# Gate-u weight jobs moved behind the first period and onto GpSimd's queue

## The chip, the cores and the metric

The kernel runs on one core of a Trainium2 chip. The metric is device time in microseconds for one execution. The engines are TensorE (PE, matrix products; its weight loads are listed apart as PEld), VectorE (DVE), ScalarE (ACT), GpSimd (POOL) and SyncE (SP). SP does nothing here but issue transfers; GpSimd issues some too. An engine works through its own instructions strictly in the order in which the program has them, and waits where an operand isn't ready.

## What is computed

A linear-attention layer with a delta rule, then a gated mixing block, then a channel block. Cut to what matters:

```python
# attention: per batch and head (4 x 8), 768 tokens, head dim 48
for t in range(S):
    y[t] = q[t] @ state
    state = state + beta[t] * outer(k_n[t], v[t] - k_n[t] @ state)
# x = y of all heads side by side: [4, 768, 384]
h = gelu(x @ w_in)                  # 384 x 1024
u, v = h[..., :512], h[..., 512:]   # "gate u" and "gate v"
v_n = layernorm(v) * g_ln
v_s = w_sg @ v_n + b_sg             # over the tokens
x = x + (u * v_s) @ w_out
xk, xr = shifted mixes of x         # mu_k, mu_r
out = sigmoid(xr @ w_r) * ((relu(xk @ w_k) ** 2) @ w_v)
```

Products that need it are done as three or four products of a high and a low part in the rounded type fp32r. So every weight matrix has to be rounded on the chip into a high and a low part before PE can use it.

## The kernel before

The attention part runs over 144 points in six periods of 24 (g = 0 to 5, 128 tokens each). A "run" is a slot of the attention and three points: after the attention steps of the slot (st_rq, st_d, st_n, st_s, st_y) `tick()` is called three times. For each period the chunk's triangular systems have to be solved first: `solver(g + 1)` is a long chain of DVE operations (from the transpose L360 over L355 and L393 to the last transpose L440, which writes DT) that runs while PE works on period g. `couple` (L456) is the first product of a new period that reads DT. `st_d` (L521) reads r, which DVE makes (L475) from what st_rq left; `st_n` reads u (ACT L526); `st_s` (L549) reads the SQ and sw0 tiles that ACT fills at L540 and L555. `warm` matmuls (L726) fill places where PE would have nothing to do.

In the gaps of DVE, ACT and POOL the weights are rounded by jobs. `narrow` is the body of a job for one block of 128 rows by 256 columns (192 for w_out): the load of `raw` (L160, issued on SP), ACT L164, four DVE operations L169, L171, L173, L175 in the tile `na`, POOL L177, ACT L120 for the high part, POOL L123 for the low part. `raw` has three buffers and `na` two, so the third job's L169 needs the first job's L123. `resident` makes such jobs for w_in, whose results stay in SBUF: six of gate v (wiv) and six of gate u (wiu), in that order. `scratch` makes the jobs of the other weights, whose results go to DRAM by one more transfer (L202) and are loaded later through GpSimd's queue (L212).

The order of all engines is made when the program is built: `background(t)` deals out a budget of DVE time at each point among three kinds of streams, layer-norm steps, the solver and jobs, in proportion to the shares in `SHARE` (one triple for the lead-in, one for the first period, one for the rest). `start_job(lead)` takes the next job off the list, issues its load and lets its operations begin `lead` points later. `tick()` starts a job where n, the point within the period, is a multiple of EVERY or, from point LATE on, of 2, as long as fewer than RUN jobs run and the point is below LASTP; and as long as w_in jobs are left (`len(jobs) > n_rest`) it starts them at any point. What is left at the end of the attention part runs beside the mixing block. `after(n, f)` puts a piece n points later. After the attention part PE does the mixing block (about 336 to 504 us) and then the channel block (504 to 745).

Of the kernel before, what the change touches and what calls it, by code (L numbers as in the profile page):

```python
# [9 lines left out]
U32 = mybir.dt.uint32  # L10
# [8 lines left out]
FF = 1024  # L19
HF = 512  # L20
P = 128
# [5 lines left out]
CW = 256  # L27
NPRE = 1.2
LJ = 2
LJ5 = 6  # L30
LJ0 = 7
SLOT0 = 3.3
LOW0 = 1
# [6 lines left out]
RUN = (3, 2, 3)  # L40
SUMS = (0,)
EVERY = 6
LATE = 100
PUT = 2
JLAG = 2
BUDGET = 1.62
# [5 lines left out]
LNW = 1  # L52
LAGX = 6
LAGE = (7, 11)
LASTP = 134
FROM = 125
LAGU = 5
COST = dict(rq=1.05, d=0.8, n=0.8, s=0.85, y=1.1)
INST = dict(rq=128, d=128, n=64, s=64, y=64)
PACE = 0.0157  # L60
SHARE = ((1, 12, 1), (1, 4, 1), (2, 8, 2))
NRAW = 3
NNA = 2
PD = 2
# [9 lines left out]
def vw(t, off, dims):  # L74

    a = t[:]
    return bass.AP(a.tensor, a.offset + off, [list(a.ap[0])] + [list(d) for d in dims])
# [9 lines left out]
def fused_kernel(  # L87
# [17 lines left out]
    nc = tc.nc  # L105
    V, A, G, T = nc.vector, nc.scalar, nc.gpsimd, nc.tensor
# [3 lines left out]
    stg = ctx.enter_context(tc.tile_pool(name="stg", bufs=2))  # L110
# [6 lines left out]
    def split(eng_hi, eng_lo, src, hi, lo):  # L117

        if eng_hi is A:
            A.activation(hi, src, AF.Copy)  # L120
        else:
            eng_hi.tensor_scalar(hi, src, 1.0, None, op0=ALU.mult)
        eng_lo.tensor_tensor(lo, src, hi.bitcast(F32), op=ALU.subtract)  # L123
# [27 lines left out]
                T.matmul(pt, lhsT=a, rhs=b, start=(i == 0), stop=(i == n - 1))  # L151
                i += 1

    def narrow(dram, i, j, hi, lo, cw=CW, pool=stg, lag=JLAG, parts=None):

        w = CW if pool is stg else cw
        raw = pool.tile([P, 2 * w], U32, name="raw", bufs=NRAW)
        nc.sync.dma_start(out=raw[:, :2 * cw], in_=dram[i * P:(i + 1) * P, j:j + cw].bitcast(U32))  # L160
        w_lo = vw(raw, 0, [(2, cw)])
        w_hi = vw(raw, 1, [(2, cw)])
        yield 0
        yield 0, lambda: A.activation(w_lo.bitcast(I32), w_lo, AF.Copy, scale=2.0 ** -29)  # L164
        a = pool.tile([P, w], U32, name="na", bufs=NNA if pool is stg else 2)[:, :cw]
        af = a.bitcast(F32)
        t1 = cw / 1920 + 0.16
        t2 = cw / 960 + 0.16
        V.tensor_scalar(a, w_hi, 0x7FFFFFFF, None, op0=ALU.bitwise_and)  # L169
        yield t1  # L170
        V.tensor_scalar(af, af, E_LO_F, E_HI_F, op0=ALU.max, op1=ALU.min)  # L171
        yield t1
        V.tensor_scalar(a, a, 3, 0x3FFFFFFF, op0=ALU.logical_shift_left, op1=ALU.bitwise_and)  # L173
        yield t1
        V.scalar_tensor_tensor(a, w_hi, 0xC0000000, a, op0=ALU.bitwise_and, op1=ALU.bitwise_or)  # L175
        yield t2
        G.tensor_tensor(a.bitcast(I32), a.bitcast(I32), w_lo.bitcast(I32), op=ALU.add)  # L177
        if hi is None:
            hi, lo = (raw[:, e * cw:e * cw + cw].bitcast(F32R) for e in range(2))
            parts.append(raw[:, :2 * cw].bitcast(F32).rearrange("p (x n) -> p x n", x=2))  # L180
        yield lag, lambda: split(A, G, af, hi, lo)

    def resident(dram, pool, name, nblk, n, j0=0, j1=None):


        j1 = j1 or n
        hi = pool.tile([P, nblk, j1 - j0], F32R, name=name + "_hi", bufs=1)
        lo = pool.tile([P, nblk, j1 - j0], F32R, name=name + "_lo", bufs=1)
        return hi, lo, [lambda i=i, j=j: narrow(dram, i, j, hi[:, i, j - j0:j - j0 + CW],
                                                lo[:, i, j - j0:j - j0 + CW], lag=0)  # L190
                        for i in range(nblk) for j in range(j0, j1, CW)]

    def scratch(dram, name, nblk, n, cw=CW, pool=stg):

        d = dp.tile([nblk, P, 2, n], F32, name=name + "_d")

        def job(i, j):
            parts = []
            yield from narrow(dram, i, j, None, None, cw, pool, parts=parts)

            def put():
                nc.sync.dma_start(out=d[i, :, :, j:j + cw], in_=parts[0])  # L202

            yield PUT, put

        return d[:, :, 0], d[:, :, 1], [lambda i=i, j=j: job(i, j) for i in range(nblk) for j in range(0, n, cw)]
# [12 lines left out]
    wo_dh, wo_dl, jobs = scratch(w_out, "wo", 4, DM, DM // 2)  # L219
    wk_dh, wk_dl, j1 = scratch(w_k, "wk", 3, FF)  # L220
    jobs += j1
    n_rest = len(jobs)
    fp = tc.tile_pool(name="fp", bufs=2)
    fl = ctx.enter_context(ExitStack())
    fp = fl.enter_context(fp)
# [23 lines left out]
    with ExitStack() as at:  # L249
        ap1 = at.enter_context(tc.tile_pool(name="ap1", bufs=1, side="right"))  # L250
        ap2 = at.enter_context(tc.tile_pool(name="ap2", bufs=2, side="right"))
        ps1 = at.enter_context(tc.tile_pool(name="ps1", bufs=1, space=PSUM))
        ps2 = at.enter_context(tc.tile_pool(name="ps2", bufs=2, space=PSUM))
        wv_hi, wv_lo, in_jobs = resident(w_in, fp, "wiv", 3, FF, HF, FF)
        wu_hi, wu_lo, j1 = resident(w_in, fp, "wiu", 3, FF, 0, HF)
        in_jobs += j1

        NKT = 5
# [61 lines left out]
        def gram(g, parts=((0, 64),)):  # L320

            GL = GLs[g] = GLb[g % 3]

            def half(i, c0, c1, j):
                t = kT[2 * g + i // 2]
                if j == 0:
                    GDs["ps"] = bank()
                gps = GDs["ps"]
                for p in range(4 * j, 4 * j + 4):
                    u = (i % 2) * 8 + p  # L330
                    for h in range(2):
                        r = 64 * (1 - h)
                        T.matmul(gps[r:r + 32, p, c0:c1], lhsT=t[r:r + 64, u, 0:32],  # L333
                                 rhs=t[r:r + 64, u, c0:c1], start=True, stop=True)
                        T.matmul(gps[r + 32:r + 64, p, c0:c1], lhsT=t[r:r + 64, u, 32:64],  # L335
                                 rhs=vw2(t, r, 64, u * C + 32 - c0, [(-32, (c1 - c0) // 32), (1, 32)]),
                                 start=True, stop=True)
                if j:
                    for x, c in ((GD[:, :, 8 * i:8 * i + 8].rearrange("p j u -> p u j"), 0),
                                 (GL[:, 8 * i:8 * i + 8, :], 32)):  # L340
                        if c0 <= c < c1:
                            A.activation(x, gps[:, :, c:c + 32], AF.Copy, scale=-1.0)

            GDs[g] = GD
            return [[(0, lambda i=i, j=j, c=c: half(i, *c, j)) for j in range(2)]
                    for c in parts for i in range(4)]
# [248 lines left out]
        later, vstat, streams, point = [], {}, [], [0, 0]  # L595
# [132 lines left out]
        def background(t):  # L728
# [8 lines left out]
            while t > 0:  # L737
# [12 lines left out]
                try:  # L750
# [7 lines left out]
                    else:  # L758
                        t -= c
                        spent[k] += c / SHARE[point[1]][k]  # L760
                    streams.remove(e)
# [6 lines left out]
        running, debt = [], [0]  # L768
        jobs = in_jobs + jobs
        n_jobs = len(jobs)  # L770

        def start_job(lead=LJ):
            j = jobs.pop(0)()
            running.append((n_jobs - len(jobs) - 1, j))
            next(j)
            streams.append([point[0] + lead, j, "job"])
# [58 lines left out]
        def tick():  # L835
            g, n = divmod(point[0], 24)
            point[1] = min(g, 1) + 1
            gg, nn = divmod(point[0] - GRAM0, 24)
            if nn == 0 and 0 <= gg and gg + 2 < NG:
                grams.extend(gram(gg + 2))  # L840
            if n == 0 and g + 1 < NG:
                streams.append([point[0] + SOLVE0, solver(g + 1), "solve"])
            late = point[0] >= LATE
            if point[0] < LASTP and jobs and len(running) < RUN[1 + late] and n % (2 if late else EVERY) == 0:
                start_job(LJ5 if late else LJ)
            background(BUDGET * (B0 if g == 0 else 1))
            while len(jobs) > n_rest and len(running) < RUN[0]:
                start_job()
            if grams and (point[0] - GRAM0) % GSTEP == 0:
                for _, f in grams.pop(0):  # L850
                    f()
                used[0] += 1.1
                dense[0] += 1
            point[0] += 1
# [110 lines left out]
    def begin(b, t, n):  # L965

        for d in range(4):
            begun[d] = (ps.tile([P, HF], F32, name="ms"), n)
        return [lambda c=c, d=d: mix_mm(begun[d][0], b, t, d, c)
                for c in range(n) for d in range(4)]  # L970
# [15 lines left out]
    parts = begin(0, 0, CS[0])  # L986
# [256 lines left out]
```

## Time and profile before

| what | us |
|---|---|
| median of 3 runs | 750.33 (748.93 to 750.84) |
| the profiled execution | 747.35 |
| span of its trace | 745.5 |
| PE busy | 690.3 (93%) |
| DVE busy | 514.1 (69%) |
| ACT busy | 367.9 (49%) |
| POOL busy | 201.6 (27%) |

The span is the time between the first and the last instruction; 1.85 us lie around it. PE is busy in nearly all of the second half, where it does only dense products; DVE's share is an average over an attention part in which it hardly rests and a last part in which it is half idle. So a share says little here, and the trace is read by stretches. Start times in the rows are microseconds from the start of the span; an operation's line number is that of the kernel before.

### The profile page before, as it was taken

Reading aid. Unit: us, or ns where it says so; the run is one execution under the profiler, and the core shown is the slowest. Engines: PE = TensorE matmul, PEld = TensorE weight load, DVE = VectorE, ACT = ScalarE, POOL = GpSimd, SP = SyncE. Lnnn points to the kernel's source line nnn. Section 1 sums busy time; section 2 is a strip of 40 time slices with the busy share of each in tenths; the row PEclk is TensorE's granted clock in tenths of the full one; section 3 lists DMA queues with packets and bytes.
Section 4 is the critical chain, followed back from the end, with each engine's and each line's share of the span. In section 5 each row is a group of like instructions: output and inputs, shape, how many; then the busy total and the mean of one; then the engine's idle time right before and its main releaser. Section 6 shows DMA issues by size and latency. Waiting matters only on the chain.

```text
span 745.5 us, 24942 instructions
## 1 busy us (share of the span) xinstructions
PE 690.3 (93%) x10832; PEld 641.5 (86%) x10832; DVE 514.1 (69%) x1070; ACT 367.9 (49%) x752; POOL 201.6 (27%) x253
## 2 busy tenths in 40 slices
PE   2668789999998999899999999999999999999998
PEld 2537568878886987779999999999999999999997
DVE  6989999898998695642476857599556565563341
ACT  2226656766675676774331413149445354452240
POOL 3033534454444265463131515330000000000000
PEclk9988989999999899999999999999999999999999
DMA  8503443575565565848763645268000000000000
GB/s 237 133 30 85 130 109 102 165 211 144 144 193 146 151 185 160 231 139 234 236 229 103 189 134 168 84 204 222 33 11 21 33 11 23 22 11 32 16 17 33
DMA packets 81550, 88.76 MB, mean 119 GB/s; under 512 B 24704, under 2 KB 64320, under 8 KB 81440
## 3 DMA queue, kind: packets, MB, share of 16 engines
q1 hardware_dynamic: 76384, 77.72, 35.2%
q0 software_dynamic: 5056, 9.44, 4.7%
q8 instruction: 85, 1.39, 0.8%
q14 instruction: 25, 0.20, 0.1%
HBM read 56.60 MB, written 25.82 MB: 111 GB/s over the span
## 4 chain that ended last, share of the span: by engine, by line
PE 74%; DVE 17%; issue 3%; ACT 2%; DMA 1%; POOL 1%; SPq 1%; POOLq 0%; DVEq 0%; ACTq 0%
PE ms L151 39%; PE ms L960 13%; PE ms L687 5%; DVE sg L355 5%; PE ms L635 4%; DVE sg L393 3%; PE ms L563 2%; DVE Yt L393 2%; PE rk L521 1%; PE ms L456 1%; PE rk L534 1%; PE sps L549 1%; PE rk L498 1%; PE ms L333 1%; PE ms L726 1%
## 5 line engine op out<-in xcount | busy, mean ns | idle before, releaser
L151 PE MATMUL ms<-wvh,sl 128*128 128x384 f32 x192 | 64.6, 336 | 0.0
L151 PE MATMUL ms<-wvl,sh 128*128 128x384 f32 x192 | 64.5, 336 | 0.0
L151 PE MATMUL ms<-wvh,sh 128*128 128x384 f32 x192 | 64.5, 336 | 0.0
L151 PE MATMUL ms<-xm_hi,sw0h 128*128 128x384 f32 x192 | 64.2, 335 | 0.0
L151 PE MATMUL ms<-xm_hi,sw0l 128*128 128x384 f32 x192 | 64.2, 334 | 0.0
L151 PE MATMUL ms<-xm_lo,sw0h 128*128 128x384 f32 x192 | 64.2, 334 | 0.0
L1059 ACT ACTIVATE gh<-w 128x384 fp32r<-128x384 f32 x32 | 16.8, 526 | 93.4 <-DVE w L1058 93.4
L177 POOL TENSOR_TENSOR na<-na,raw 128x256 int32<-128x256 int32 (+2 forms) x43 | 36.5, 849 | 96.0 <-ACT gh L1059 40.7
L123 DVE TENSOR_TENSOR sl<-sg,sh 128x384 fp32r<-128x384 f32 x64 | 35.7, 558 | 30.2 <-ACT sh L120 30.2
L120 ACT ACTIVATE sh<-sg 128x384 fp32r<-128x384 f32 x64 | 33.5, 524 | 36.4 <-DVE sg L1163 36.4
L960 PE MATMUL ms<-sw0h,g 128*128 128x384 f32 x192 | 50.2, 335 | 0.0
L960 PE MATMUL ms<-ws1h,g 128*128 128x384 f32 x192 | 49.9, 334 | 0.0
L355 DVE TENSOR_TENSOR sg<-sg,Yt 128x512 f32<-128x512 f32 (+10 forms) x78 | 46.8, 599 | 1.8
L1179 DVE TENSOR_TENSOR sg<-sg,ms 128x384 f32<-128x384 f32 x24 | 13.3, 555 | 44.9 <-PE ms L151 44.9
L1163 DVE TENSOR_TENSOR sg<-sg 128x384 f32<-128x384 f32 x64 | 35.4, 553 | 10.9 <-ACT sg L1162 10.9
L1162 ACT ACTIVATE sg<-ms 128x384 f32<-128x384 f32 x64 | 30.7, 480 | 22.9 <-PE ms L151 22.9
L514 POOL TENSOR_SCALAR_AFFINE_SELECT SQ<-SQ 64x512 f32<-64x512 f32 x36 | 27.0, 749 | 50.9 <-ACT SQ L513 49.8
L120 ACT ACTIVATE xm_hi<-sg 128x384 fp32r<-128x384 f32 x48 | 23.1, 517 | 34.6 <-PE ms L151 30.5
L687 PE MATMUL ms<-xl,wiu_hi 128*128 128x256 f32 x144 | 39.7, 297 | 0.0
L687 PE MATMUL ms<-xh,wiu_lo 128*128 128x256 f32 x144 | 38.7, 292 | 0.1
L333 PEld LDWEIGHTS ms<-kT 64*32 64x32 f32 x640 | 20.0, 131 | 21.7 <-issue 13.9
L335 PE MATMUL ms<-kT 64*32 64x64 f32 (+1 forms) x640 | 23.3, 235 | 16.5 <-issue 16.5
(246 smaller groups left out, 2241.1 us busy)
## 6 DMA issues: line engine op xcount, KB each, us to landing
u_d<-ug SPq DMA_DIRECT2D x24, 256.0 KB, 4.6
u<-u_d SPq DMA_DIRECT2D x16, 384.0 KB, 4.3
vn_d<-v SPq DMA_DIRECT2D x22, 256.0 KB, 2.8
vk<-in_vk_dram SPq DMA_DIRECT2D x24, 192.0 KB, 3.6
vk<-in_vk_dram SPq DMA_DIRECT2D x12, 384.0 KB, 4.5
out_dram<-sg SPq DMA_DIRECT2D x24, 192.0 KB, 1.9
kT<-in_kt_d_dram SPq DMA_DIRECT2D x8, 512.0 KB
SQ<-in_q_d_dram SPq DMA_DIRECT2D x36, 96.0 KB, 4.0
```

What stands on the lines that cost most here:

```text
L120: A.activation(hi, src, AF.Copy)
L123: eng_lo.tensor_tensor(lo, src, hi.bitcast(F32), op=ALU.subtract)
L151: T.matmul(pt, lhsT=a, rhs=b, start=(i == 0), stop=(i == n - 1))
L177: G.tensor_tensor(a.bitcast(I32), a.bitcast(I32), w_lo.bitcast(I32), op=ALU.add)
L333: T.matmul(gps[r:r + 32, p, c0:c1], lhsT=t[r:r + 64, u, 0:32], rhs=t[r:r + 64, u, c0:c1], start=True, stop=True)
L355: V.tensor_tensor(tv, vw(a_t, a_off, a_dims), vw(b_t, b_off, b_dims), op=ALU.mult)
L393: V.tensor_reduce(out=o_ap, in_=tv, axis=AX.X, op=ALU.add)
L635: T.matmul(vstat[g, b], lhsT=a[:, c], rhs=w[:, c], start=first, stop=last)
L687: T.matmul(vstat["u"][:, 2 * P * d:2 * P * d + 2 * P], lhsT=w[:, c, ds_], rhs=a[:, c].rearrange("p b t -> p (b t)"), start=first, stop=last)
L960: T.matmul(pt[:, :DM], lhsT=v[:, ds_], rhs=w, start=(c == 0 and i == 0), stop=(c == 5 and i == 2))
L1162: A.activation(r, pt[:, :DM], AF.Relu)
L1163: V.tensor_tensor(r, r, r, op=ALU.mult)
```

## The change

Five numbers change: LJ5 from 6 to 5 (points between load and first operation of a late job), LATE from 100 to 96 (from here a job may start every second point), LASTP from 134 to 142 (no job starts behind it), the share of the first period from (1, 4, 1) to (1, 8, 1) (layer norm, solver, jobs), and a new LJU = 3. The six gate-u jobs get their load from GpSimd instead of SP. `tick()` starts other jobs only from the third period on (g > 1), and up to point 14 it leaves the six gate-u jobs in the list, so in that stretch only gate-v jobs start; from point 15 on gate-u jobs start, three points between load and first operation.

```diff
-LJ5 = 6
+LJ5 = 5
-LATE = 100
+LATE = 96
+LJU = 3
-LASTP = 134
+LASTP = 142
-SHARE = ((1, 12, 1), (1, 4, 1), (2, 8, 2))
+SHARE = ((1, 12, 1), (1, 8, 1), (2, 8, 2))
@@ narrow
-        nc.sync.dma_start(out=raw[:, :2 * cw], in_=dram[i * P:(i + 1) * P, j:j + cw].bitcast(U32))
+        (eng or nc.sync).dma_start(out=raw[:, :2 * cw], in_=dram[i * P:(i + 1) * P, j:j + cw].bitcast(U32))
@@ attention part
-        wu_hi, wu_lo, j1 = resident(w_in, fp, "wiu", 3, FF, 0, HF)
+        wu_hi, wu_lo, j1 = resident(w_in, fp, "wiu", 3, FF, 0, HF, G)
@@ tick
-            if point[0] < LASTP and jobs and len(running) < RUN[1 + late] and n % (2 if late else EVERY) == 0:
+            if g > 1 and point[0] < LASTP and jobs and len(running) < RUN[1 + late] and n % (2 if late else EVERY) == 0:
                 start_job(LJ5 if late else LJ)
             background(BUDGET * (B0 if g == 0 else 1))
-            while len(jobs) > n_rest and len(running) < RUN[0]:
-                start_job()
+            while len(jobs) > n_rest + (0 if point[0] > 14 else 6) and len(running) < RUN[0]:
+                start_job(LJU)
```

PE's order stays the same row for row. DVE, ACT and POOL have the same operations in another order, and six loads go from SP's queue to POOL's. The changed file is one line longer from line 43 on, so L440 of before is L441 there.

DVE at the end of solver 1 and the start of solver 2 (L360, in the changed kernel L361). Before:

```order
L355 TENSOR_TENSOR sg_111<-sg_110,Yt 128x1024
L171 TENSOR_SCALAR na<-na 128x256
L393 TENSOR_REDUCE sg_110<-sg_111 128x4x16
L173 TENSOR_SCALAR na<-na 128x256
L440 STREAM_TRANSPOSE DT<-sg_110 128x32x32
L169 TENSOR_SCALAR na<-raw 128x256
L175 SCALAR_TENSOR_TENSOR na<-raw,na 128x256
L475 TENSOR_TENSOR r_1642<-vk,rk 128x384
```

And in the changed kernel, from the row behind DT's transpose on:

```order
L172 TENSOR_SCALAR na<-na 128x256 x2
L174 TENSOR_SCALAR na<-na 128x256 x2
L176 SCALAR_TENSOR_TENSOR na<-raw,na 128x256 x2
L170 TENSOR_SCALAR na<-raw 128x256
L172 TENSOR_SCALAR na<-na 128x256
L174 TENSOR_SCALAR na<-na 128x256
L176 SCALAR_TENSOR_TENSOR na<-raw,na 128x256
L476 TENSOR_TENSOR r_1624<-vk,rk 128x384
L170 TENSOR_SCALAR na<-raw 128x256 x2
L172 TENSOR_SCALAR na<-na 128x256 x2
L174 TENSOR_SCALAR na<-na 128x256 x2
L361 STREAM_TRANSPOSE sg_108<-sg_109 128x1024
```

The gate-u jobs, of which four of six had gone through DVE ahead of DT before, now stand behind DT, three of them ahead of r and parts of two more between r and the start of solver 2.

ACT in the same place, from the eviction of y (L568) to the eviction of the couple product (L459); L540 fills the matrices that step s reads. Before:

```order
L568 ACTIVATE yst<-ms 128x8x64
L120 ACTIVATE wiu_hi<-na 128x256
L164 ACTIVATE raw<-raw 128x256
L540 ACTIVATE SQ_127<-rk 64x8x48
L540 ACTIVATE SQ_128<-rk 64x8x48
L513 ACTIVATE sw0h_121<-qk 64x8x64
L513 ACTIVATE sw0l_122<-qk 64x8x64
L120 ACTIVATE wiu_hi<-na 128x256 x2
L459 ACTIVATE sw0h_113<-ms 32x512 x2
```

And in the changed kernel:

```order
L569 ACTIVATE yst<-ms 128x8x64
L121 ACTIVATE wiu_hi<-na 128x256 x2
L165 ACTIVATE raw<-raw 128x256
L121 ACTIVATE wiu_hi<-na 128x256
L541 ACTIVATE SQ_127<-rk 64x8x48
L541 ACTIVATE SQ_128<-rk 64x8x48
L514 ACTIVATE sw0h_121<-qk 64x8x64
L514 ACTIVATE sw0l_122<-qk 64x8x64
L460 ACTIVATE sw0h_113<-ms 32x512 x2
```

Ahead of the two L540 (L541) stands now the high part of three jobs, where it was one.

POOL in the same place, where `vk` (L465) is the scaling of the next tokens. Before:

```order
L465 TENSOR_TENSOR vk<-vk,neT 128x768
L177 TENSOR_TENSOR na<-na,raw 128x256
L123 TENSOR_TENSOR wiu_lo<-na,wiu_hi 128x256
L514 AFFINE_SELECT sw0h_121<-sw0h_121 64x8x64
L514 AFFINE_SELECT sw0l_122<-sw0l_122 64x8x64
```

And in the changed kernel:

```order
L466 TENSOR_TENSOR vk<-vk,neT 128x768
L178 TENSOR_TENSOR na<-na,raw 128x256
L124 TENSOR_TENSOR wiu_lo<-na,wiu_hi 128x256
L178 TENSOR_TENSOR na<-na,raw 128x256
L124 TENSOR_TENSOR wiu_lo<-na,wiu_hi 128x256
L161 DMA raw<-in_w_in_dram 128x512 x2
L178 TENSOR_TENSOR na<-na,raw 128x256
L124 TENSOR_TENSOR wiu_lo<-na,wiu_hi 128x256
L161 DMA raw<-in_w_in_dram 128x512
```

Between the two low parts of jobs 2 and 3 POOL now issues the loads of jobs 4 and 5, and after that the load of job 6.

## Rows read from the trace of the kernel before

**Rows 1.** Windows: busy us (instructions) per engine, granted clock, DMA share, GB/s.

```profile
52.90:95.30 42.40, 34.11 (x1113) 25.45 (x1111) 41.16 (x90) 25.58 (x56) 19.45 (x23) 0.86 0.37 104
95.30:143.10 47.80, 45.84 (x1372) 37.49 (x1372) 44.33 (x96) 31.89 (x62) 20.25 (x25) 0.95 0.45 124
```

**Rows 2.** PE's waits, 0 to 250: who waits, for whom: us in total, times, longest.

```profile
PE ms L456 <- DVE na L169: 4.3, 1, 4.3
...
PE ms L456 <- DVE sw0l L440: 3.6, 1, 3.6
```

**Rows 3.** Chain of work that ended last, 95 to 145: start us, us, what.

```profile
95.47 1.92 PE ms L456 x64
97.38 1.82 PE ms L726 x4
99.20 1.32 PE rk L521 x64
100.52 0.85 PE sps L549 x32
...
106.28 1.13 PE ms L456 x64
...
111.86 0.81 PE rk L521 x64
```

**Rows 4.** VectorE's groups, 54.25 to 93.3: busy us, mean ns, idle before.

```profile
L171 DVE TENSOR_SCALAR na<-na 128x256 f32<-128x256 f32 x5 | 3.5, 697 | 0.0
...
L175 DVE SCALAR_TENSOR_TENSOR na<-raw,na 128x256 uint32<-128x256 uint32 x6 | 3.0, 493 | 0.0
L169 DVE TENSOR_SCALAR na<-raw 128x256 uint32<-128x256 uint32 x5 | 2.7, 549 | 0.0
L173 DVE TENSOR_SCALAR na<-na 128x256 uint32<-128x256 uint32 x5 | 2.0, 403 | 0.0
```

**Rows 5.** Timeline of VectorE: start us, us, line, operation, tiles [idle before].

```profile
93.07 0.42 DVE L173 TENSOR_SCALAR na<-na 128x256 uint32<-128x256 uint32 x1
93.41 1.91 DVE L440 STREAM_TRANSPOSE DT<-sg 128x1024 f32<-128x1024 f32 x1
...
97.49 1.24 DVE L360 STREAM_TRANSPOSE sg<-sg 128x1024 f32<-128x1024 f32 x1
...
108.94 0.54 DVE L475 TENSOR_TENSOR r<-vk,rk 128x384 f32<-128x384 f32 x1
```

**Rows 6.** Timeline of ScalarE at 91 us.

```profile
91.01 0.99 ACT L540 ACTIVATE SQ<-rk 64x384 f32<-64x384 f32 x2
```

**Rows 7.** Timeline of GpSimd, two stretches.

```profile
89.41 0.79 POOL L177 TENSOR_TENSOR na<-na,raw 128x256 int32<-128x256 int32 x1
...
99.38 0.72 POOL L123 TENSOR_TENSOR wiu_lo<-na,wiu_hi 128x256 fp32r<-128x256 f32 x1 [0.53 <-ACT wiu_hi L120]
...
346.73 0.80 POOL L212 DMA_DIRECT2D wo_hi<-wo_d  x1
```

**Rows 8.** List of DMA issues: KB each, median us to landing.

```profile
wr_lo<-wr_d POOLq DMA_DIRECT2D x1, 576.0 KB, 9.9
```

**Rows 9.** All loads issued by L160, on SP's queue.

```profile
DMA to landing us min/median/max: 2.6/4.2/5.1
```

**Rows 10.** Timeline of GpSimd, 108 to 118.

```profile
112.44 1.70 POOL L465 TENSOR_TENSOR vk<-vk,neT 128x768 f32<-128x768 f32 x1 [5.01 <-DMA vk<-in_vk_dram]
116.09 1.68 POOL L123 TENSOR_TENSOR xl<-xT,xh 128x768 fp32r<-128x768 f32 x1 [1.94 <-ACT xh L120]
```

**Rows 11.** PE's waits, 250 to 745.

```profile
PE rk L521 <- DVE r L475: 1.5, 2, 1.3
PE ms L635 <- ACT GL L459: 1.3, 1, 1.3
```

**Rows 12.** Tile wr_lo: ns min/median/max, first and last start.

```profile
L151 PEld LDWEIGHTS ms<-wr_lo,xm_hi x72: 187/188/188, 516.4 to 737.2; 128*128 128x128 f32 x72
...
L212 POOL DMA_DIRECT2D wr_lo<-wr_d x1: 767/767/767, 504.9 to 504.9; - x1
```

More of the change, by code (lines that the diff above doesn't have):

```diff
@@ L152, in mm3, with narrow @@
                 i += 1
-    def narrow(dram, i, j, hi, lo, cw=CW, pool=stg, lag=JLAG, parts=None):
+    def narrow(dram, i, j, hi, lo, cw=CW, pool=stg, lag=JLAG, parts=None, eng=None):
         w = CW if pool is stg else cw
         raw = pool.tile([P, 2 * w], U32, name="raw", bufs=NRAW)
-        nc.sync.dma_start(out=raw[:, :2 * cw], in_=dram[i * P:(i + 1) * P, j:j + cw].bitcast(U32))
+        (eng or nc.sync).dma_start(out=raw[:, :2 * cw], in_=dram[i * P:(i + 1) * P, j:j + cw].bitcast(U32))
         w_lo = vw(raw, 0, [(2, cw)])
@@ L181, in narrow, with resident @@
         yield lag, lambda: split(A, G, af, hi, lo)
-    def resident(dram, pool, name, nblk, n, j0=0, j1=None):
+    def resident(dram, pool, name, nblk, n, j0=0, j1=None, eng=None):
         j1 = j1 or n
@@ L189, in resident @@
         return hi, lo, [lambda i=i, j=j: narrow(dram, i, j, hi[:, i, j - j0:j - j0 + CW],
-                                                lo[:, i, j - j0:j - j0 + CW], lag=0)
+                                                lo[:, i, j - j0:j - j0 + CW], lag=0, eng=eng)
                         for i in range(nblk) for j in range(j0, j1, CW)]
```

## The prediction

> **What bounds the kernel now.** I read the table of windows first, to see in which stretch TensorE (PE) isn't busy; then PE's waits, for what it lacked there; then the chain of work that ended last across that place; then the timelines of VectorE (DVE), ScalarE (ACT) and GpSimd (POOL) around it. From 95.30 on PE is nearly full, 45.84 of 47.80 us; from 52.90 to 95.30 it works 34.11 of 42.40, at a granted clock of 0.86 [rows 1]. One of its longest waits before 250 us is that of the couple matmuls (L456), 4.3 us [rows 2]: they start at 95.47 [rows 3], so PE had been ready since 91.17. What they lack is DT, the result of the solver on DVE, whose last transpose starts at 93.41 and takes 1.91 [rows 5]. In this solver's window DVE also does 21 operations of w_in jobs, 11.2 us in all [rows 4]. Behind the wait PE runs slowly: the same 64 couple matmuls take 1.92 us there and 1.13 later, the 64 of step d 1.32 and 0.81 [rows 3].
>
> **What the change takes away.** Four of the 21 job operations stay ahead of DT: two of L175 and two of L169. So 11.2 − 2 × 0.49 − 2 × 0.55 = 9.1 us leave [rows 4]. Records of neighbours overlap by about 0.08 us (L173 ends at 93.49, the transpose starts at 93.41 [rows 5]), 17 × 0.08 = 1.4, so DT comes 7.7 us earlier: the transpose runs from 85.7 to 87.6. That is ahead of 91.17, where PE takes over as the bound. Worth by itself: 4.3 us of waiting, 0.79 + 0.51 us of slow couple and d, and 0.75 for the warm-up matmuls between them, if their 1.82 shrinks as couple does [rows 3]. Together 6.3 us, the upper end.
>
> **What it puts in its place.** PE's own order doesn't change by a row; only its operands' times move. Three things now stand in the way, worked on from DT at 87.6.
>
> First, ACT and POOL. DVE does the rest of jobs 1 and 2 behind DT (two each of L171, L173, L175; about 0.3, 0.3 and 0.4 where nothing slows them), the first L175 ending at 89.2. Each job then goes to POOL (L177, 0.79), ACT (L120, 0.4, and 0.1 for the hand-over) and POOL (L123, 0.72 in its shortest row) [rows 7]: 90.0, 90.5, 91.3 for the first, 92.1, 92.6, 93.4 for the second. POOL then issues two loads, at 0.80 each as an issue at 346.73 shows [rows 7]: 95.0. L177 of job 3 ends at 95.8, its L120 at 96.3. Behind three such L120 in ACT's queue stand the two L540 that put n into the matrices of step s, 0.99 [rows 6]; before, one stood there. So PE gets to s of this pair at about 97. It is ready for it at 94.2 (91.17 + 1.13 + 1.07 + 0.81) and reached it at 100.52 [rows 3]. Of the 6.3 us 3.5 are left, and PE has a new wait of nearly 3.
>
> Second, DVE and the loads. Two gate-u jobs (the fourth and fifth, L169, L171, L173) now stand in DVE's queue ahead of the first operation of solver 2, the transpose L360. Their loads go out behind POOL's work, at 94.2 and 95.0. With the 4.2 us that loads of this line took by SP [rows 9] they land at 98.4 and 99.2; the second L169 and the two pairs behind it take 0.3 + 0.6 + 0.6, and solver 2 starts at 100.7 instead of 97.49 [rows 5]. The r of the next step d stood 11.45 us behind L360, at 108.94; five solver operations ahead of it (1.4 us) change place with four job operations (1.1), so it comes 11.15 behind, at 111.9, is done at 112.4, and d starts then, where before it started at 111.86 [rows 3]. Where POOL issues in 0.3 us less and L123 always takes 0.72 it is up to 1 us less. The lead of 3.5 us is then between −0.6 and +0.4.
>
> Third, ACT and POOL again. The sixth job's L177 stands on POOL behind L465, which waited until 112.44 for the load of vk, and its L120 on ACT stands ahead of v, u and xh. The split of x on POOL (L123, 1.68) that the gate-u matmuls need starts at 116.09 before [rows 10]. vk's load is issued a fixed run of SP's issues after s, so L465 starts 3.5 us earlier, at 108.9, and ends at 110.6; L177 at 111.4, L120 at 111.8; from there ACT does the table load, v, u, the evictions and xh, some 5 us by the same operations of before, and the split starts at 116 to 117: no lead, up to 1 us late. Both leashes say the same, so I book **0** for the second period, not −6.3.
>
> The bounds of this term: no row shows a 256 KB load from POOL's queue. By SP, loads of this line landed between 2.6 and 5.1 us [rows 9]; POOL's own of 576 KB takes 9.9 [rows 8]. I take 4.2, the median for the same transfer. At 2.6 the second leash gives 1.6 us more lead, at 9.9 it takes 5.7.
>
> The rows put POOL's 576 KB at 9.9 us [rows 8]. The Trainium skill, page "DMA: Bandwidth & Descriptors", section "Anatomy of one DMA — SWDGE (gpsimd) path", fits a GpSimd DMA as about 2.0 us plus bytes over 436e3: about 2.6 us for 256 KB, by which the second leash alone would lie near +1.5 us of lead. The trace speaks against it: for 576 KB the fit gives 3.4.
>
> **The rest of the change.** Solver 2 has 6 job operations in it instead of 11, so it starts later and ends about as before, ahead of its couple: 0. The third period's order is the same. In the fourth, the solver meets 192-wide jobs where before three were 256 wide, 12 operations at some 0.05 less each: **−0.6** of the wait of 3.6 us on its L440 [rows 2]. Solver 5 likewise, with less in it: **−0.2**. In the last attention window a job (four operations, 1.4 us) now stands ahead of r in two places where PE already waited for r, 1.5 us in sum; right behind them PE waits 1.3 for an eviction by ACT [rows 11], which takes up part: **+0.4**, bounds 0 and 1.5. One more w_k job runs beside the mix stage and the last w_v job moves to its end. The latest of the loads behind it, wr_lo, is issued at 504.9, takes 9.9 [rows 8] and is first used at 516.4 [rows 12]: 1.6 us to spare, which I take to hold: 0, bounds 0 and 1. SP loses six issues: nothing that PE waits for.
>
> **The sum.** 0 − 0.6 − 0.2 + 0.4 = −0.4 us on the profiled 747.35. That execution lies 2.98 below the median of 750.33, so for the median: 749.9.
>
> **Rivals.** *A, the gain comes through.* The loads land in about 3 us, and POOL works faster once DVE isn't filled with jobs; both leashes give way by 2 to 3 us. For it: the wait of 4.3 us is certain to go, and the durations of POOL were read beside a DVE full of jobs. Against it: two separate queues, ACT's and DVE's, would have to be faster than their rows. It gives −3.1 − 0.4, 746.8; at most −6.3, 744.
>
> *B, slower: POOL's loads come late.* The loads gate solver 2, and through it r and d. From a landing of about 4.2 us on, each further microsecond is one on PE. With 7 us it is +2.8 − 0.4, and couple's 0.8 again for the low clock behind a long wait [rows 3]: +3.2, 753.5; with 9.9 about 756. For it: POOL's row of 9.9, and that DVE works without a pause at that time. Against it: those loads are more than twice as large.
>
> The row of 9.9 stands for this rival [rows 8]. The Trainium skill, page "SBUF — State Buffer", in its box on how DVE blocks a GpSimd DMA, says that such a DMA's descriptors can't be written while DVE holds the port that both share, and puts one at about 0.62 us alone and 3.1 beside a copy: 2.5 us more, by which this leash would give about +2.5 us. No row shows a w_in load in that queue.
>
> *C, slower: the tail.* The last w_v job moves past its 1.6 us and the tiles come 2 to 4 us late at the start of the last stage: +2.5, 752.8. Against it: four short operations move, not a transfer's length.
>
> **How the numbers follow.** A measurement of this kernel tells about 0.3%, 2.25 us, from no change. The forecast (the gain eaten by new waits, 748.1 to 752.5) has 0.50, A 0.27, B 0.15, C 0.08. Faster is A, 0.27; same 0.50; slower B and C, 0.23. The range takes the forecast's own and the near parts of A, B and C: 746.0 to 753.5 leaves the far ends of A and B out, about 0.2.
>
> **What the profile will show.** Right: no wait of couple for DT near 91; a new wait of s from about 94 to 97 that leads over ACT's L540 and L120 to POOL; L360 of solver 2 at 99 to 101; the next d within 1 us of 111.9; a wait near 240 of about 3 us. If L360 starts before 98.5 and s before 95.5, A holds. If d comes at 114 or later and DVE's L169 waited for a load, B holds. Wrong altogether: DT still late at the first couple, or waits in PE's last stage that weren't there.

## The result and the profile after

The changed kernel is slower. Beside each other the runs gave 758.36 us (755.78 to 758.74) against 749.63 (744.90 to 750.84), a ratio of 1.0121 with an interval of 1.0071 to 1.0171. Among the experiments, on another chip, it was 755.03 against 746.61, 1.0112 (1.0078 to 1.0145). So it costs some 8 to 9 us where 749.9 had been forecast, and the time lies outside the range. Single runs of one kernel spread over 3 to 11 us, so the experiments are compared by their ratios to the kernel before on the same chip; a single profile is used for places, not for totals.

The profiled execution took 755.78 us, with a span of 754.0, 8.5 longer than before. Line numbers are one higher than before.

The table of windows of the changed kernel, the stretches of [rows 1] (columns as there):

```profile
52.90:95.30 42.40, 36.04 (x1176) 26.92 (x1171) 36.68 (x82) 21.86 (x46) 17.16 (x23) 0.87 0.36 88
95.30:143.10 47.80, 41.90 (x1319) 34.14 (x1319) 42.40 (x88) 31.90 (x63) 21.58 (x26) 1.00 0.46 131
```

The first stretch got fuller by 1.9 us, as it should when the wait of couple goes; the second has 3.9 us less of PE work, part of it because the granted clock is 1.00 there and was 0.95, but also 53 instructions fewer (1319 for 1372). The gain is given back right behind the place where it arises.

PE's waits of the changed kernel (us in total, times, longest), the answer to [rows 2, 11]:

```profile
PE ms L457 <- DVE sw0l L441: 3.7, 1, 3.7
...
PE rk L522 <- DVE r L476: 2.9, 1, 2.9
...
PE ms L152 <- DMA wr_lo<-wr_d: 2.1, 1, 2.1
PE ms L564 <- POOL var L665: 1.9, 1, 1.9
```

The 4.3 us of couple for L169 behind a late DT are gone. Three waits are new: step d for r in the second period, the last stage for wr_lo, and the last step y for a layer-norm operation on POOL. The wait near 240 is 3.7.

VectorE's timeline of the changed kernel, from DT to the r of the second period (start us, us, line, operation, in brackets the idle time before and what ended it), the answer to [rows 5]:

```profile
85.38 1.97 DVE L441 STREAM_TRANSPOSE DT<-sg 128x1024 f32<-128x1024 f32 x1
...
92.04 0.82 DVE L170 TENSOR_SCALAR na<-raw 128x256 uint32<-128x256 uint32 x1 [3.30 <-POOL wiu_lo L124]
...
97.47 0.29 DVE L170 TENSOR_SCALAR na<-raw 128x256 uint32<-128x256 uint32 x1 [2.63 <-DMA raw<-in_w_in_dram]
98.55 0.33 DVE L170 TENSOR_SCALAR na<-raw 128x256 uint32<-128x256 uint32 x1 [0.78 <-DMA raw<-in_w_in_dram]
...
100.26 1.23 DVE L361 STREAM_TRANSPOSE sg<-sg 128x1024 f32<-128x1024 f32 x1
...
103.07 1.71 DVE L139 TENSOR_TENSOR rn_t<-rn_y 128x32 f32<-128x32 f32 x1
...
111.60 1.53 DVE L356 TENSOR_TENSOR sg<-sg,Yt 128x64 f32<-128x64 f32 x1
113.06 0.54 DVE L476 TENSOR_TENSOR r<-vk,rk 128x384 f32<-128x384 f32 x1
```

DVE, which hardly rested here before, stands still for 3.30 + 2.63 + 0.78 = 6.7 us: once because `na` has two buffers and job 3 needs job 1's, twice for loads. Solver 2 starts 2.8 us later than before although DT came 8 us earlier.

ScalarE and GpSimd of the changed kernel, in one timeline of each, where the last of the gate-u jobs stands:

```profile
116.31 0.42 ACT L121 ACTIVATE wiu_hi<-na 128x256 fp32r<-128x256 f32 x1 [4.10 <-POOL na L178]
116.75 1.28 ACT L645 ACT_TABLE_LOAD   x1
118.05 0.60 ACT L645 ACTIVATE v<-ms 128x512 f32<-128x512 f32 x1
```

```profile
115.49 0.79 POOL L178 TENSOR_TENSOR na<-na,raw 128x256 int32<-128x256 int32 x1 [2.43 <-DVE na L176]
...
121.33 1.67 POOL L124 TENSOR_TENSOR xl<-xT,xh 128x768 fp32r<-128x768 f32 x1 [3.46 <-ACT xh L121]
```

ACT stands still for 4.1 us ahead of an operation of that job, with the table load and v behind it; the split of x, at 116.09 before [rows 10], starts at 121.33. What the job waits for is not the load of vk but its own DVE operation, queued in solver 2 behind r.

GpSimd, the landing of wr_lo (KB, us) and the windows of the changed kernel at the start of the last stage:

```profile
503.36 1.19 POOL L124 TENSOR_TENSOR raw<-na,raw 128x384 fp32r<-128x384 f32 x1 [0.64 <-ACT raw L121]
507.42 0.95 POOL L1126 DMA_DIRECT2D wvh<-wv_d  x1 [2.88 <-DMA wv_d<-raw]
508.37 0.88 POOL L1126 DMA_DIRECT2D wvl<-wv_d  x1
509.25 0.75 POOL L213 DMA_DIRECT2D wr_hi<-wr_d  x1
509.98 0.77 POOL L213 DMA_DIRECT2D wr_lo<-wr_d  x1
```

```profile
wr_lo<-wr_d POOLq DMA_DIRECT2D x1, 576.0 KB, 13.4
```

```profile
518.00:524.00 6.00, 3.85 (x23) 3.54 (x22) 6.00 (x14) 5.99 (x14) 0.00 (x0) 1.00 0.87 212
524.00:530.00 6.00, 6.00 (x27) 6.00 (x26) 6.00 (x14) 5.05 (x11) 0.00 (x0) 0.72 0.00 1
```

The last w_v job ends on POOL at 503.36 + 1.19; its store holds the whole queue until 507.42. The four loads then leave within 3.3 us, where before w_v had a lead of 3 us on w_r; wr_lo takes 13.4 us to land, not 9.9 [rows 8], and PE starts with it at 523.47. Behind this wait PE runs six microseconds at a granted clock of 0.72: 27 matmuls there, where the next 10 us hold 60, or 36 in six, so about 1.5 us more.

PE's order is the same in both kernels, so the same step can be looked up in both traces; the difference of their starts tells where the time goes. For the changed kernel's two profiles against that of before:

| step of PE | before | changed | again |
|---|---|---|---|
| couple behind DT | 95.47 | −1.8 | −5.8 |
| next d (L521) | 111.79 | +1.9 | +2.4 |
| n behind it (L534) | 118.39 | +2.7 | +3.9 |
| couple of period 5 | 287.77 | +1.3 | +1.3 |
| first product of the last stage | 503.9 | +3.8 | +2.8 |
| first with w_v | 518.0 | +7.0 | +6.1 |
| last with w_v | 741.3 | +8.6 | +6.1 |

Two places stand out: from 95 to 118, and from 504 to 525. Between them PE gains a little and loses it again, which the part on the prediction takes up. Starts in the 35 us before 95 differ between executions by up to 2.8 us either way, by waits that the profile puts down to "issue"; 23.1 us of them in the profile before, 20.7 to 29.0 in the thirteen profiles of this study, with no pattern by kernel. Waits for DVE further on take such differences up again, so a difference of 1 or 2 us between two single profiles shows nothing.

### The profile page after: what moved, and what is told of

Read it like the earlier page. It is cut to its first block, busy times and chain, and to the rows that moved or that the text cites. A ratio compares the mean times of both kernels' runs of the same rounds, so it can differ in the third digit from the quotient of the medians.

```text
span 754.0 us, 24933 instructions
## 1 busy us (share of the span) xinstructions
PE 693.9 (92%) x10832; PEld 644.9 (86%) x10832; DVE 511.9 (68%) x1070; ACT 368.4 (49%) x752; POOL 204.7 (27%) x259
## 4 chain that ended last, share of the span: by engine, by line
PE 70%; DVE 14%; DMA 6%; issue 3%; POOL 3%; ACT 2%; SPq 1%; POOLq 0%; DVEq 0%; ACTq 0%
PE ms L152 35%; PE ms L961 11%; PE ms L688 7%; PE ms L636 5%; DVE sg L356 4%; PE ms L564 2%; DVE sg L394 2%; DMA wr_lo<-wr_d 2%; PE sps L550 2%; PE rk L522 2%; DVE Yt L394 1%; PE rk L535 1%; PE rk L499 1%; DMA raw<-in_w_in_dram 1%; PE ms L334 1%
## 5 line engine op out<-in xcount | busy, mean ns | idle before, releaser
L178 POOL TENSOR_TENSOR na<-na,raw 128x256 int32<-128x256 int32 (+2 forms) x43 | 36.1, 839 | 94.0 <-ACT gh L1060 41.0
L121 ACT ACTIVATE sh<-sg 128x384 fp32r<-128x384 f32 x64 | 33.5, 524 | 35.4 <-DVE sg L1164 35.4
L356 DVE TENSOR_TENSOR sg<-sg,Yt 128x512 f32<-128x512 f32 (+10 forms) x78 | 45.2, 579 | 1.9
L121 ACT ACTIVATE xm_hi<-sg 128x384 fp32r<-128x384 f32 x48 | 23.3, 518 | 34.7 <-PE ms L152 30.5
L688 PE MATMUL ms<-xh,wiu_hi 128*128 128x256 f32 x144 | 38.7, 292 | 0.0
```

The source lines that it names most:

```text
L356: V.tensor_tensor(tv, vw(a_t, a_off, a_dims), vw(b_t, b_off, b_dims), op=ALU.mult)
L688: T.matmul(vstat["u"][:, 2 * P * d:2 * P * d + 2 * P], lhsT=w[:, c, ds_], rhs=a[:, c].rearrange("p b t -> p (b t)"), start=first, stop=last)
```

## Experiments

Theory T: two separate costs, the gate-u jobs between DT and the gate-u matmuls, and the last weight job at the end of the mixing block. Rivals put the whole down to one of them, to GpSimd's queue, or to the clock.

**The loads back on SP** (`sp_loads`).

```diff
-        wu_hi, wu_lo, j1 = resident(w_in, fp, "wiu", 3, FF, 0, HF, G)
+        wu_hi, wu_lo, j1 = resident(w_in, fp, "wiu", 3, FF, 0, HF)
```

> The changed kernel with one thing undone: the six gate-u loads go out by SP again; all orders of operations stay. Theory T (two separate costs: about 4.5 us at the start of the last stage, where wr_lo comes late, and about 4 us in the attention part, from the order of the gate-u jobs and not from the queue of their loads): the loads save at most the 3.4 us for which DVE waits on them, most of it covered, so 756 to 758, with the wait on wr_lo unchanged. Rival R (GpSimd's queue is the cause in the attention part, by late loads and by what they do to the other transfers): 753 to 755, and PE's waits marked issue, 6 us more than before in the changed kernel, fall back to about 23 us.

It took 757.09 us, ratio 1.0169 (1.0100 to 1.0237), no faster than the changed kernel. VectorE in this run:

```profile
97.90 0.29 DVE L170 TENSOR_SCALAR na<-raw 128x256 uint32<-128x256 uint32 x1 [3.56 <-DMA raw<-in_w_in_dram]
...
99.89 1.23 DVE L361 STREAM_TRANSPOSE sg<-sg 128x1024 f32<-128x1024 f32 x1
...
113.44 0.55 DVE L476 TENSOR_TENSOR r<-vk,rk 128x384 f32<-128x384 f32 x1
```

The wait for the load is as long from SP, and solver 2 starts within 0.4 us of the same time. So GpSimd's queue as such isn't the cause, and rival R falls. The run doesn't show that the time of the issue is indifferent, though. SP's timeline in this run:

```profile
90.59 3.43 SPq L589 DMA_DIRECT2D xT<-yst  x4
94.12 2.37 SPq L161 DMA_DIRECT2D raw<-in_w_in_dram  x3
```

The loads stand behind other transfers of SP and leave at 94.12, as late as from GpSimd (94.04 in the changed kernel), although the first job's L178, the last to read the buffer that the fourth job's load fills, had ended at 90.25. Either queue lets that load out some 3 to 4 us after its buffer is free; no run tried it earlier. The waits on issue came to 25.7 us; this run settles nothing on them.

**The two halves apart** (`first_only`, `late_only`). The first keeps the gate-u part, the second the numbers of the later periods:

```diff
# first_only, against the changed kernel
-LJ5 = 5
-LATE = 96
-LASTP = 142
+LJ5 = 6
+LATE = 100
+LASTP = 134
-            if g > 1 and point[0] < LASTP
+            if g > 0 and point[0] < LASTP
# late_only, against the kernel before
-LJ5 = 6
-LATE = 100
-LASTP = 134
+LJ5 = 5
+LATE = 96
+LASTP = 142
-            if point[0] < LASTP
+            if g > 1 and point[0] < LASTP
```

> Only the first-period part of the change: gate-u jobs late and by GpSimd, the share of 8; LJ5, LATE and LASTP as before, and other jobs may start from the second period on (g > 0) instead of the third. As many jobs are left beside the mixing block as before (12). Theory T: the tail cost is gone and the cost of the attention part stays: 752.5 to 754.5, no wait on wr_lo. Rival R2 (the late jobs cost nothing by themselves, the 8.7 us come from the first period alone): 757 to 759.

> Only the other part: the first period as in the kernel before, and LJ5 = 5, LATE = 96, LASTP = 142 and other jobs from the third period only. 14 jobs are left beside the mixing block, where it was 12. Theory T: wr_lo waits for the store of the last w_v job and lands 2 us late, with a low clock behind it: 753.5 to 755, wait on wr_lo about 2 us. Rival R2: 749 to 751.

Measured: first_only 752.37, ratio 1.0084 (1.0056 to 1.0112); late_only 751.99, ratio 1.0077 (1.0039 to 1.0115). Each half costs about 6 us, so neither alone is the cause; the two together cost 8 to 9, so they don't simply add up. In late_only d and n of the second period are 0.9 us earlier than before, the last stage begins 0.8 later and its w_v part 3.8 later, with

```profile
PE ms L151 <- DMA wr_lo<-wr_d: 1.9, 1, 1.9
```

In first_only n of the second period is 5.6 later, and there is no wait in the last stage. It is no clean half, though: with g > 0 solver 2 takes 18 job operations (11 before, 6 in the changed kernel), and PE loses 4.4 us more up to 150. The next run looks at the gate-u part by itself.

**Half of the gate-u work left out** (`half_jobs_skipped`). In `narrow`, for the last three gate-u jobs:

```diff
+        if skip:
+            for t in (cw / 1920, cw / 1920, cw / 1920, cw / 960):
+                yield t + 0.16
+            yield lag, lambda: split(A, G, w_hi.bitcast(F32), hi, lo)
+            return
```

> The changed kernel, but the last three gate-u jobs leave out the exact rounding: ACT's L165, the four DVE operations and POOL's L178 aren't there, the raw high words are split as they are. So part of the computation is missing. Everything else keeps its order. Theory T2 (DVE's job operations between DT and solver 2, their waits on the loads, and L178 of the last job behind DVE's queue set the second period): solver 2's first transpose starts at 95 to 96 instead of 100.3, the first r of the second period at 106 to 108 instead of 113.1, d there waits for nothing, PE reaches n of that pair 4 us or more earlier than in the changed kernel, and the run is about 5 us faster than it: 3 to 4 us over the kernel before. Rival (the chain of the first three jobs over POOL and ACT to step s costs as much by itself): d of the second pair still at 112 or later, no faster than the changed kernel by more than 2 us.

748.58 us, ratio 1.0024 (0.9998 to 1.0050), 6 us under the changed kernel. VectorE in this run (line numbers are six higher):

```profile
87.13 1.94 DVE L447 STREAM_TRANSPOSE DT<-sg 128x1024 f32<-128x1024 f32 x1
...
94.57 0.54 DVE L482 TENSOR_TENSOR r<-vk,rk 128x384 f32<-128x384 f32 x1
95.04 1.23 DVE L367 STREAM_TRANSPOSE sg<-sg 128x1024 f32<-128x1024 f32 x1
105.78 0.54 DVE L482 TENSOR_TENSOR r<-vk,rk 128x384 f32<-128x384 f32 x1
```

Solver 2 at 95.04 and r at 105.78, 10.7 us behind it, as T2 has it; d waits for nothing, and n starts 1.0 us before that of the kernel before. The rival, by which the first three jobs alone cost as much, falls. The run takes away the work of three jobs and with it DVE's waits for their loads, so it doesn't tell one from the other. It does tell what the wait of 4.3 us was worth: even with the work of three jobs gone, PE gains 1.0 there (1.6 against the mean of the five profiles with the old first period, which lie at 0, −0.9, +2.2, −0.1 and +1.6).

**Three jobs before DT, three behind** (`three_early`).

```diff
-            while len(jobs) > n_rest + (0 if point[0] > 14 else 6) and len(running) < RUN[0]:
+            while len(jobs) > n_rest + (0 if point[0] > 14 else 3) and len(running) < RUN[0]:
-            if g > 1 and point[0] < LASTP
+            if point[0] >= 32 and point[0] < LASTP
```

> The changed kernel with three of the six gate-u jobs let in from the start of the first period (10 of their operations inside solver 1 instead of 4, where it was 21 before), and other jobs from point 32 on, so that as many are left beside the mixing block as before (12). Theory T2: DT comes at about 90, ahead of 91.2, solver 2 starts at 97 to 98 and the tail is as before: the time is within 2 us of the kernel before, on the faster side if step s isn't late. Rival (any gate-u job behind DT costs as all six do): 4 us or more over it.

749.48 us, ratio 1.0038 (1.0009 to 1.0067), 3 us over before: between what the two expected. Solver 2 started at 99.22 and r at 112.03, still behind two waits of DVE for loads, but n of the second period is only 0.8 us later than before, where the profiles with the old first period lie at 0.6 on the mean. The place is eased, then; this profile loses its time behind it, 5.6 us between 118 and the last stage, and no run tells why. Inconclusive on the size.

**The tail by doses** (`late_free`, `no_first_two`). Both are the kernel before; one has LJ5 = 5, LATE = 96 and LASTP = 142 alone (11 jobs left beside the mixing block, 12 before), the other only `g > 1` (15 left; 14 in the changed kernel).

> The kernel before with LJ5 = 5, LATE = 96 and LASTP = 142 alone; other jobs start in every period as before. 11 jobs are left beside the mixing block (12 before, 14 in the changed kernel). Theory T: no wait on wr_lo, so nothing of the 4.6 us of the tail: within 2 us of the kernel before. Rival (the late window itself costs, by jobs ahead of r): 3 to 5 us over it, with r waits near 302 and 315 of 3 us or more.

> The kernel before with other jobs from the third period on alone (g > 1); 15 jobs are left beside the mixing block. Theory T: the last w_v store comes still later than with 14 jobs, so the wait on wr_lo grows from 2.1 to 4 us or more, and the time is 6 to 9 us over the kernel before. Rival (the tail depends on where the last job happens to fall, not on how many are left): 0 to 4 us over it.

late_free: 747.44, ratio 1.0007 (0.9988 to 1.0025), no wait in the last stage. no_first_two: 759.25, ratio 1.0153 (1.0111 to 1.0195), although PE was 2.4 us earlier than before at the end of the attention part. Its waits behind 330:

```profile
PE ms L151 <- ACT xm_hi L120: 10.7, 1, 10.7
```

ACT in the same run, at the operand that PE waits for:

```profile
511.86 1.35 ACT L120 ACTIVATE xm_hi<-sg 128x384 fp32r<-128x384 f32 x3 [5.72 <-DMA wv_d<-raw]
```

So 11 and 12 jobs cost nothing, 14 cost a wait of 2 us on wr_lo, and with 15 the operand of the stage's first product (xm_hi) itself waits for the store of the last job. T foresaw the growth, but neither its size (13 us for the 6 to 9 expected) nor that the wait would change its place.

**The end of the queue** (`wr_first`, `after_side3`, `late_side3`). The first moves the w_v loads behind those of w_r in the code, the others set SD from 2 to 3, which gives the jobs beside the mixing block up to three operations per unit, so the last job's DVE work is done three of 32 units earlier.

> The changed kernel with the two w_v loads moved behind the two w_r loads in GpSimd's queue at the start of the last stage; nothing else. Theory T: w_r is needed first (521) and lands by 519, w_v is needed at 525 and lands by 521 to 523: the wait of 2.1 us and the 1.7 us of low clock behind it go, 753.5 to 755. Rival R3 (the time behind 518 is lost to the clock or to contention and not to this wait): 757 to 759, with the matmuls of the last stage as slow as now.

> The changed kernel with SD = 3 instead of 2: up to three job operations per unit of the mixing block, so the last w_v job has done its DVE work three of 32 units before the end instead of at the end. Theory T: the wait on wr_lo and the low clock behind it go, 4 to 5 us off the changed kernel, 4 to 5 us over the kernel before. Rival (the tail's time is lost to the two more jobs themselves, which only move): within 2 us of the changed kernel.

> The later half of the change (first period as before; LJ5 = 5, LATE = 96, LASTP = 142, other jobs from the third period only) with SD = 3. In the run with SD = 2 PE was 0.8 us earlier than in the kernel before at the end of the attention part, 3 us earlier at 290, and lost 4.6 at the tail. Theory T: the tail's loss goes: 0 to 2 us under the kernel before. Rival (three operations per unit hold up DVE's part of the mixing block): 1 to 4 us over it, with waits of PE in the stretch from 336 to 504.

wr_first: 752.68, ratio 1.0100 (1.0068 to 1.0133), no clear gain on the changed kernel's 1.0112. POOL issued wvh, wr_hi, wr_lo, wvl there, so only one of the two w_v loads moved behind those of w_r: the wait on wr_lo is gone, and PE waited 1.0 for wvl and 0.5 for xm_hi instead. Between 504 and 540 PE loses 2.2 us in this profile, where the two of the changed kernel lose 4.8 and 3.3. The order of the loads isn't the root; all of them come late.

after_side3: 750.65, ratio 1.0049 (1.0023 to 1.0074), against 1.0112 for the unchanged one: 0.63%, 4.7 us. The tail is a cost by itself, and giving the same jobs their time earlier takes most of it away; in the profile 1.1 us of the wait on wr_lo are left, at full clock. late_side3: 748.98, ratio 1.0024 (1.0000 to 1.0048), 4 us less than late_only, but not under the kernel before, as T had hoped; that lies in the range of the rival. Nothing there says that the mixing block suffers: PE's only waits of over 0.5 us from 330 on are 2.0 for the layer-norm step on POOL and 0.9 for wr_lo.

**The changed kernel again** (`after_again`).

> The changed kernel as it is, on the same chip as the others, to have its distance from the kernel before beside theirs. Both theories: 1.010 to 1.014 of it, 753.5 to 757 where the kernel before takes 746.2.

755.03, ratio 1.0112, as told above. Its wait on wr_lo was 2.2 us, and in the windows behind it PE ran at full clock: the low clock after this wait came in one profile of two.

No version beat the kernel before; late_free is level with it.

## Why the prediction was wrong

*Right.* The first couple no longer waits for DT: the transpose ran from 85.38 to 87.35, against 85.7 to 87.6. The chain over POOL and ACT to step s: L121 of job 3 began at 95.96 (95.9 by the working) and the two L541 ended at 97.39 (97.3). PE had itself lost 1.4 us to issue there, so that in this profile it waited for neither. In the second profile it waited 0.5 us for L541, and 2.9 ahead of it for the r that stands behind job 3 on DVE; the forecast had named the place and the jobs, but of this r it had no term. The loads landed at 97.4 and 98.5 for 98.4 and 99.2. Solver 2 at 100.26 for 100.7. So the gain was eaten right behind the first couple, as said, and rival A was rightly held small. Rival B had the right place and the wrong cause: these loads landed in 3.3 to 3.8 us, less than the 4.2 assumed. By the prediction's own sign (d at 114 or later, and a wait of L170 for a load) B would hold in the second profile, where d starts at 114.20, so that sign doesn't tell the two apart.

*The second leash, mis-sized by 1.2 us, and without the clock behind its wait.* r was put 11.15 us behind the start of solver 2 and stood 12.8 behind it (113.06). In that stretch two short solver operations took 1.71 and 1.53 us instead of about 0.2; each ends with a POOL operation beside it, the split of x (103.04 to 104.73) and vk (111.58 to 113.05). That the one holds up the other is read from these times; no run moved them apart. Before, one such stretch fell on the solver ahead of its r and the other on a job, as VectorE's timeline of the kernel before shows:

```profile
104.17 1.54 DVE L355 TENSOR_TENSOR sg<-sg,Yt 128x4 f32<-128x4 f32 x1
...
112.73 1.53 DVE L169 TENSOR_SCALAR na<-raw 128x192 uint32<-128x192 uint32 x1
```

The step took the solver's length over from there, without the question which of its operations would now meet POOL's.

PE then waits for this r at d, 2.5 to 5.4 us in the six profiles that have the whole gate-u part. In five of them it runs slowly behind the wait, as the windows show, first of the changed kernel's first profile, then of its second:

```profile
114.00:118.00 4.00, 4.00 (x122) 3.26 (x109) 3.78 (x11) 1.67 (x2) 1.85 (x2) 1.00 0.08 25
114.00:118.00 4.00, 3.80 (x119) 3.59 (x121) 3.79 (x14) 1.13 (x2) 1.44 (x2) 0.58 0.11 39
```

From d to the end of y the same products take 2.75 us in the first profile, 4.20 in the second (114.20 to 118.40) and 4.2 to 4.8 in the other four. That is some 1.5 us or more on top of the wait. The forecast charged a low clock (0.8) only in rival B and put it at nothing in its own sum.

*The third leash, a wrong wait that decided little.* The working took the sixth job's L177 to wait for L465 and vk, and let ACT go on at 111.8. Its own last DVE operation stands behind r in solver 2, at 115.00, and so the L121 that should have ended at 111.8 ended at 116.73. The orders of ACT and POOL alone don't show that; DVE's beyond r does. In the first profile PE waits for what comes behind it on ACT, v:

```profile
PE ms L334 <- ACT v L645: 0.6, 1, 0.6
```

In the other five PE reaches that product 0.8 to 1.4 us after v is done (119.99 against 119.18 in the second), held by the slow stretch, and doesn't wait. So at d the six profiles are 2.5 us late on the mean, against 0.5 for the five with the old first period, and at n 4.0 (2.7 to 5.6) against 0.6. Where the step was booked at 0 (−0.6 to +0.4 of lead) it measured 3.5 us: 2.1 by the late r, and 1.4 on the mean behind it, by the low clock in five profiles (1.5 to 2.1) and by v in the one where the clock stayed up (0.9).

*The tail, booked at 0 with a bound of 1.* "One more w_k job" was a miscount: two more jobs are left, 14 for 12. "Four short operations move" was the wrong unit: a job is a chain over DVE, POOL, ACT, POOL and a store, and its end on POOL moved from 497.29 to 504.55, 7.3 us, with PE's start of the stage 3.8 later. GpSimd's timeline of the kernel before, for the last low part and the first load:

```profile
496.00 1.29 POOL L123 TENSOR_TENSOR raw<-na,raw 128x384 fp32r<-128x384 f32 x1 [3.52 <-ACT raw L120]
500.17 0.95 POOL L1125 DMA_DIRECT2D wvh<-wv_d  x1 [2.88 <-PE ms L151]
```

There the first load waited for PE, after the change for the store. The spare 1.6 us [rows 8, 12] was right, and smaller than the move. I also took the 9.9 us of wr_lo as given; with its three neighbours in front of it within 3.3 us it took 13.4. Cost: 3.0 to 4.8 us in the five profiles with 14 jobs left, SD = 2 and the loads in this order, 4.7 by after_side3. Rival C had the mechanism, at 2.5 us and 0.08; it decided half of the result.

*The rest, booked at −0.4.* The wait near 240 is 3.7 us in the first profile for 3.6 before, and 0.5 in the second, where PE comes to it later; the gain of 0.6 by lighter jobs can't be read from either. From 118 to 250 PE gains 1.3 to 3.5 us against the profile before in ten of the twelve other profiles, also in those that have the old first period or the old late numbers, so there it is the one profile before that is slow. From 250 to the mixing block PE loses 1.4 to 3.9 in the nine profiles with LASTP = 142 whose other jobs start only from point 32 or 48 on; the four others lie between −1.2 and 0. The forecast had +0.4 there, bounds 0 and 1.5. One wait in this stretch it missed altogether, on GpSimd behind a late job's two operations, as its timeline of the changed kernel shows:

```profile
335.98 0.73 POOL L178 TENSOR_TENSOR na<-na,raw 128x256 int32<-128x256 int32 x1
337.24 0.72 POOL L124 TENSOR_TENSOR raw<-na,raw 128x256 fp32r<-128x256 f32 x1 [0.53 <-ACT raw L121]
338.05 0.23 POOL L665 TENSOR_SCALAR var<-mv 128x2 f32<-128x2 f32 x1
```

PE waits 1.9 us for the last of these, a layer-norm step. Gain and loss come out near 0 against the one profile before; that they do so in the time isn't shown.

So by the profiles the late r and the clock behind it cost 3.5 us and the tail 3.3 to 4.8, with a rest near 0, where 8.4 to 8.7 were measured. The tail has its own run: after_side3 takes 0.63% off, and its interval (1.0023 to 1.0074) lies below that of the changed kernel (1.0078 to 1.0145). The first-period part is shown to cost by half_jobs_skipped, but its size is less sure: the two pairs of runs that differ in it alone, the changed kernel against late_only and after_side3 against late_side3, give 0.35 and 0.25%, 2 to 3 us, each within some 3 to 4 us either way. late_side3 with its 0.24% leaves up to 2 us for the late jobs in the attention part. How the first period and these late jobs share some 4 us stays open, and the share of the first period, (1, 8, 1), was never changed alone.

## What to carry to other kernels

A wait of 4 us on the chain isn't worth 4 us: first see what is next late for the same engine, and for work that is only moved, find the queue it lands in and what stands behind it on *each* engine, to the last operation of the last job. Count in whole jobs, from load to store, and ask of the last one in a stage what its store releases. A new wait can cost more than its length: behind that for r PE's granted clock fell, for 1.5 us more. Where a background chain feeds a stage by a queue, its end is a cliff: 12 jobs cost nothing, 14 cost 4 us, 15 some 13.

## What was not expected of the hardware

Loads of 256 KB from GpSimd's queue landed in 4.0 us as a median (3.3 to 6.8; the slowest were those issued three in a row), about as long as by SP (4.2 in the profile before, 5.2 for SP's in this one); the 9.9 us of wr_lo, which had two loads of 1536 KB ahead of it, were no guide to them. Three issues in a row cost GpSimd 1.87 us, 0.6 each, less than the 0.8 assumed. And a low clock behind a wait isn't certain: behind 2.1 to 2.2 us on wr_lo it was 0.72 for six microseconds in one profile of the changed kernel and full in the other, and behind the wait for r it was the other way round, full after 2.9 us and 0.58 for four microseconds after 2.5.
